# Two clearings on GpSimd ahead of its first load, and a shorter spin on TensorE

## The chip, the cores and the metric

The kernel runs on one core of one Trainium2 chip. A core has TensorE (PE, matrix products; PEld is its loading of stationary operands), VectorE (DVE), ScalarE (ACT), GpSimd (POOL) and SyncE (SP), and sixteen DMA engines that move data between the device's memory and the core. The metric is device microseconds from the first to the last instruction, as the median of repeated executions. Lower is better.

## The reference, cut to what matters

Eight batches of twelve heads with 448 rows of 64 elements go through an attention without softmax: the scores are scaled, negative ones are cut to zero, and the rest is squared. The heads, side by side, are the 3584 x 768 input of a two-layer network with an exact GELU.

```
scores = q @ k.T / sqrt(64)
attn   = maximum(scores, 0) ** 2 / 448
x      = (attn @ v) with the 12 heads side by side     # 3584 x 768
h      = x @ w_in                                      # 3584 x 2048
g      = 0.5 * h * (1 + erf(h / sqrt(2)))
out    = g @ w_out                                     # 3584 x 768
```

Inputs and output are float32; the kernel computes in bfloat16 with float32 sums.

## The kernel before, in words

Batches follow each other. For each, queries and keys are loaded and converted to bfloat16 (tiles `nq`, `nk`), transposed (`qT`, `kT`), multiplied to scores (line 623, tile `ps`), cut to zero (635 on ScalarE, 637 on VectorE) and squared (644), multiplied with V (683, `pav`), and copied as the network's input (`xT`). The first layer (line 730) ends in GELU on ScalarE (740), the second is at 1036 and 1131. Parts of both layers use Strassen's seven products in place of eight; their sums are formed on VectorE. Twelve heads are worked on in three groups of four.

The order of the work is fixed when the program is built. Operations are entered with durations and dependences in a planner (`Scheduler`), the first 270 placements are spelled out in the string `ORDER`, and the rest is placed by the planner; after the call of `manual_schedule` (line 1198) every engine runs its instructions in that order. No number of the planner is touched by the change. What is emitted before line 1198, the preamble that the change edits, is put in order by the framework.

Loads come in two kinds. Almost all are issued by GpSimd[...]. Batch 0 starts differently: the keys of its first head group (`k32`) are loaded as float32 by a DMA issued from ScalarE (line 1181), and half the queries of that group (`q32`) by one from SyncE (1182). ScalarE and VectorE then convert them (lines 387 and 389; in the profile the tiles stand as `k` and `q`). GpSimd's own loads start with the second group: K of group 1, half the queries of group 1, V of group 0, K of group 2, half the queries of group 2, V of groups 1 and 2, the other half of all queries, and then the first pieces of `w_in` (lines 1201 to 1208 enter them, lines 421, 336 and 439 issue them).

Ahead of that stands a preamble. A tile `zero` is cleared, a 128 x 128 identity `ident` is made for the transposes on TensorE (cleared on VectorE at line 1185, its diagonal set by GpSimd's select at 1186), ScalarE's GELU table is loaded with a dummy activation (1193), and TensorE multiplies `zero` by itself 45 times (1197, `SPIN`). These products have no reader; they keep TensorE active until the first data arrive. The transposes of keys are on line 517, those of queries on line 545. The pool `opool` has three buffers of 128 x 768 float32 under the tag `osb`, which hold output rows before they are stored.

Of the kernel before, what the change touches and what calls it, by code (L numbers as in the profile page):

```python
# [8 lines left out]
F32 = mybir.dt.float32  # L9
# [13 lines left out]
DM = H * D  # L23
# [41 lines left out]

COLD_END = 0.0
K_CUT = 4
SPIN = 45


ORDER = """
# [212 lines left out]
def kernel(  # L284
# [9 lines left out]
    nc = tc.nc  # L294
# [3 lines left out]
    def pool(name, bufs, space=None):  # L298
        if space is None:
            return ctx.enter_context(tc.tile_pool(name=name, bufs=bufs))  # L300
        return ctx.enter_context(tc.tile_pool(name=name, bufs=bufs, space=space))
# [11 lines left out]
    opool = pool("opool", 3)  # L313
# [58 lines left out]
    ident = const.tile([128, 128], BF16, tag="ident", name="ident")  # L372
# [10 lines left out]
    V, A = nc.vector, nc.scalar  # L383
# [785 lines left out]
    def slots(b, done):  # L1169
# [12 lines left out]
    nc.sync.dma_start(q32, q_view(0, 0, 1, 0, HC))  # L1182
    zero = const.tile([128, 128], BF16, tag="zero", name="zero")
    V.memset(zero, 0.0)
    V.memset(ident, 0.0)
    nc.gpsimd.affine_select(
        out=ident, in_=ident, compare_op=mybir.AluOpType.not_equal, fill=1.0,
        base=0, pattern=[[-1, 128]], channel_multiplier=1,
    )
    warm = const.tile([128, 1], F32, tag="warm", name="warm")  # L1190
    V.memset(warm, 0.0)

# [2 lines left out]
    spin = w_pp.tile([128, 2, NB], F32, tag="w", name="spin")  # L1195
    for _ in range(SPIN):
        nc.tensor.matmul(spin[:, 0, :128], zero, zero, start=True, stop=True)
# [187 lines left out]
```

## Time and profile before

| | before |
|---|---|
| time, median of 3 | 376.12 us (375.93 to 377.31) |
| span of the profiled execution | 374.2 us |
| TensorE busy | 363.0 us, 97% |
| VectorE busy | 284.3 us, 76% |
| ScalarE busy | 200.9 us, 54% |
| GpSimd busy | 46.0 us, 12% |
| HBM read, written | 45.61 MB, 11.01 MB |

The page gives the busy time of each engine, the span in 40 slices, the DMA queues, and the chain of waits: the work that ended last, followed backwards from the last instruction, at each step to what released it. In a timeline each line has the start in microseconds, the duration, the engine, the line of the code, the operation, what it writes and reads with its shape, and how often. In brackets at the end stands how long the engine was idle before, and what ended that. A table of windows gives, for each stretch of time, the busy time of the engines, then TensorE's granted clock, the busy share of the DMA engines, and the gigabytes per second that they moved.

### The profile page before, as it was taken

How to read it: one execution, taken by the hardware profiler on the slowest of the kernel's cores; microseconds unless marked ns; L12 is line 12 of the kernel's file. 1: busy time of each engine (PE TensorE's matmuls, PEld its weight loads, DVE VectorE, ACT ScalarE, POOL GpSimd, SP SyncE). 2: the span in 40 equal slices, each digit the busy share in tenths (PEclk: the TensorE clock that was granted, in tenths of full speed). 3: DMA queues.
4: the chain of work that ended last, by engine and by line, in shares of the span. 5: the costliest groups of instructions: out<-in, count | busy, mean ns of one | idle time of the engine just before them, and what ended most of it. 6: DMA issues, size and time to landing. Idle time of an engine off the chain costs nothing.

```text
span 374.2 us, 8324 instructions
## 1 busy us (share of the span) xinstructions
PE 363.0 (97%) x3485; PEld 215.4 (58%) x3485; DVE 284.3 (76%) x517; ACT 200.9 (54%) x301; POOL 46.0 (12%) x69
## 2 busy tenths in 40 slices
PE   8799999999999999999999999999999999999995
PEld 7566645455554455544555445544555886688663
DVE  3998981799848787985889768946888879785762
ACT  4998864746337865666546575657562333035100
POOL 8666400300002011002000020000000000000000
PEclk9999999999999999999999999999999999999999
DMA  9999999997579969989333799400020201210233
GB/s 175 195 201 204 202 190 114 171 205 143 94 171 162 146 75 190 238 113 159 64 101 79 140 154 181 120 3 0 2 86 12 75 2 31 90 49 2 85 86 84
DMA packets 69685, 42.96 MB, mean 115 GB/s; under 512 B 37776, under 2 KB 66192, under 8 KB 69648
## 3 DMA queue, kind: packets, MB, share of 16 engines
q0 software_dynamic: 30512, 22.47, 40.2%
q1 hardware_dynamic: 38768, 19.46, 25.5%
q8 instruction: 27, 0.44, 0.5%
q10 hardware_dynamic: 368, 0.51, 0.4%
q14 instruction: 10, 0.08, 0.1%
HBM read 45.61 MB, written 11.01 MB: 151 GB/s over the span
## 4 chain that ended last, share of the span: by engine, by line
PE 84%; DVE 6%; ACT 4%; issue 2%; DMA 2%; POOL 1%; DVEq 0%; ACTq 0%; POOLq 0%
PE pso L1036 32%; PE psh L730 29%; PE ps L623 8%; PE pb L870 7%; PE pav L683 4%; ACT a_sq L635 4%; PE pso L1131 3%; DVE a_sq L644 3%; DVE part L904 2%; DMA nk<-in_k_dram 2%; DVE a_sq L637 1%; DVE xT L387 0%; DVE kT L387 0%; PE tp L517 0%; ACT xT L389 0%
## 5 line engine op out<-in xcount | busy, mean ns | idle before, releaser
L635 ACT ACTIVATE a_sq<-ps 128x896 bf16<-128x896 f32 (+1 forms) x143 | 122.8, 914 | 57.5 <-PE ps L623 57.5
L730 PE MATMUL psh<-xT,win_sb 128*128 128x448 bf16 (+1 forms) x612 | 114.2, 342 | 0.1
L644 DVE TENSOR_TENSOR a_sq<-a_sq 128x896 bf16<-128x896 bf16 (+1 forms) x169 | 98.7, 615 | 11.2 <-ACT a_sq L635 10.1
L730 PEld LDWEIGHTS <-win_sb 128*128 128x128 bf16 x612 | 57.4, 98 | 53.7 <-issue 9.2
L740 ACT ACTIVATE h_sb<-psh 128x448 bf16<-128x448 f32 x96 | 52.5, 547 | 34.3 <-PE psh L730 34.0
L1036 PEld LDWEIGHTS <-s_sb 128*128 128x128 bf16 x424 | 40.6, 98 | 27.7 <-issue 2.5
L623 PE MATMUL ps<-qT,kT 64*64 64x448 bf16 (+1 forms) x756 | 48.5, 336 | 3.1 <-ACT a_sq L635 0.7
L637 DVE TENSOR_SCALAR a_sq<-ps 128x896 bf16<-128x896 f32 x26 | 28.2, 1088 | 28.5 <-PE ps L623 28.1
L1036 PEld LDWEIGHTS <-h_sb 128*128 128x128 bf16 x312 | 29.8, 98 | 20.9 <-issue 2.4
L1036 PE MATMUL pso<-wout_sb,h_sb 128*128 128x384 bf16 x208 | 38.1, 326 | 0.0
L1036 PE MATMUL pso<-t_sb,s_sb 128*128 128x384 bf16 x208 | 38.1, 326 | 0.0
L1036 PE MATMUL pso<-wout_sb,s_sb 128*128 128x384 bf16 (+2 forms) x216 | 38.1, 320 | 0.0
L683 PE MATMUL pav<-a_sq,v_sb 64*64 64x448 bf16 (+1 forms) x756 | 36.8, 330 | 0.8 <-ACT a_sq L635 0.4
L623 PEld LDWEIGHTS <-kT 64*64 64x64 bf16 x756 | 18.6, 105 | 26.9 <-issue 21.3
L1070 DVE TENSOR_TENSOR osb<-pso,p_sb 128x384 f32<-128x384 f32 x39 | 21.6, 555 | 9.5 <-PE pso L1036 7.3
L683 PEld LDWEIGHTS <-v_sb 64*64 64x64 bf16 x756 | 21.1, 107 | 13.1 <-issue 2.3
L387 DVE CAST xT<-pav 128x448 bf16<-128x448 f32 (+1 forms) x44 | 24.3, 582 | 5.5 <-PE pav L683 4.9
L904 DVE TENSOR_TENSOR part<-pb,part 128x448 f32<-128x448 f32 x40 | 23.1, 618 | 6.3 <-PE pb L870 6.2
L913 ACT ACTIVATE h_sb<-part 128x448 bf16<-128x448 f32 x24 | 13.3, 577 | 18.4 <-DVE part L904 18.3
L590 POOL COPY gate<-qT 128x4 bf16<-128x4 bf16 x5 | 1.3, 266 | 155.6 <-DMA qT<-pq 155.6
L870 PEld LDWEIGHTS <-win_sb 128*128 128x128 bf16 x192 | 18.4, 98 | 3.2 <-issue 2.1
L1036 PE MATMUL pso<-t_sb,h_sb 128*128 128x384 bf16 x104 | 19.0, 326 | 0.0
(60 smaller groups left out, 262.1 us busy)
## 6 DMA issues: line engine op xcount, KB each, us to landing
nk<-in_k_dram POOLq DMA_DIRECT2D x5, 672.0 KB, 6.7
nq<-in_q_dram POOLq DMA_DIRECT2D x5, 672.0 KB, 9.3
v_sb<-in_v_dram POOLq DMA_DIRECT2D x5, 672.0 KB, 13.4
out_dram<-osb SPq DMA_DIRECT2D x8, 336.0 KB, 3.1
wout_sb<-in_moe_w_out_dram POOLq DMA_DIRECT2D x2, 1152.0 KB, 11.7
v_sb<-in_v_dram POOLq DMA_DIRECT2D x9, 224.0 KB, 9.0
out_dram<-osb SPq DMA_DIRECT2D x7, 288.0 KB, 3.1
out_dram<-osb SPq DMA_DIRECT2D x8, 240.0 KB, 2.8
```

What stands on the lines that cost most here:

```text
L387: V.tensor_copy(dst, src)
L623: nc.tensor.matmul(ps[64 * j : 64 * j + 64, e, x * w : x * w + w], kT[r, g, i * 128 + 64 * j : i * 128 + 64 * j + 64], qT[r, 2 * g + j, co ...
L635: A.activation(ar, ps, AF.Relu, scale=c_att)
L637: V.tensor_scalar(ar, ps, c_att, 0.0, op0=mybir.AluOpType.mult, op1=mybir.AluOpType.max,)
L644: V.tensor_mul(box["a2"][:, :, :used], ar, ar)
L683: nc.tensor.matmul(pav[0][o2 : o2 + 64, e, :w], vt[b][r, 2 * g + e, bass.ts(i, D)], box["a2"][r, e, o : o + w], start=(i == 0), stop=(i == ...
L730: nc.tensor.matmul(ph[:, x * n : x * n + n], win_sb[:, kd, bass.ts(m + x, 128)], xT[b][:, kd, c], start=(kd == 0), stop=(kd == KD - 1),)
L740: A.activation(h_ring()[:, m : m + nm, o + c.start : o + c.stop], box[0][:, :S].rearrange("p (x n) -> p x n", x=nm), AF.Gelu,)
L870: nc.tensor.matmul(bank[name][:, y, z * HS : z * HS + HS], w[:, k, bass.ts(mm, 128)], right()[:, k], start=first and k == 0 and z == 0, st ...
L904: V.tensor_add(get(to), ps(name), get(other))
L1036: nc.tensor.matmul(box[bank][:, n0:n1], left()[:, kf], right[:, kf, n0:n1], start=bool(need) and kf == 0, stop=kf == K2 - 1, skip_group_ch ...
L1070: V.tensor_add(out()[:, n0:n1], box[bank][:, n0:n1], other()[:, n0:n1])
```

## The change

The identity is cleared on GpSimd instead of VectorE. After the identity is made, GpSimd also clears a 128 x 768 float32 tile that takes one of the three output buffers; nothing reads it. Since GpSimd works in order, its first load can only be issued after these instructions. The spin on TensorE has 37 products instead of 45. The aim is to leave the DMA engines at first to the two loads issued by ScalarE and SyncE, which the first transposes wait for, and to fit the spin to the arrival of their data.

```diff
-SPIN = 45
+SPIN = 37
...
     zero = const.tile([128, 128], BF16, tag="zero", name="zero")
     V.memset(zero, 0.0)
-    V.memset(ident, 0.0)
+    nc.gpsimd.memset(ident, 0.0)
     nc.gpsimd.affine_select(
         out=ident, in_=ident, compare_op=mybir.AluOpType.not_equal, fill=1.0,
         base=0, pattern=[[-1, 128]], channel_multiplier=1,
     )
+    first = opool.tile([128, DM], F32, tag="osb", name="osb")
+    nc.gpsimd.memset(first, 0.0)
```

## The prediction

> **What bounds the kernel now.** I read the page first: which engine is busy, and what ended the time before. Columns of the first two lines: busy time, share of the span, instructions; then busy tenths in 40 slices.
>
> ```profile
> PE 363.0 (97%) x3485; PEld 215.4 (58%) x3485; DVE 284.3 (76%) x517; ACT 200.9 (54%) x301; POOL 46.0 (12%) x69
> PE   8799999999999999999999999999999999999995
> ...
> PE 84%; DVE 6%; ACT 4%; issue 2%; DMA 2%; POOL 1%; DVEq 0%; ACTq 0%; POOLq 0%
> ```
>
> TensorE fills the span except at the two ends, so a change in the first 3 us can only move the beginning; what it moves there is carried by a nearly full TensorE to the end. So I went to the chain of waits for the first 30 us (start, length, what):
>
> ```profile
> 1.26 0.80 POOL nk L421
> ...
> 2.14 0.31 POOL ident L1186
> 2.45 0.67 POOL nq L336
> 3.12 0.69 POOL v_sb L439
> 3.81 5.92 DMA nk<-in_k_dram
> 9.73 0.04 issue
> 9.77 0.60 PE tp L517 x14
> 10.37 0.02 issue
> 10.40 0.62 DVE kT L387
> 11.02 2.98 DVE a_sq L644 x6
> ```
>
> The end hangs on the GpSimd loads: the fourth (K of the third head group, issued at 3.81) lands at 9.73, TensorE transposes it, VectorE copies it and then works without a gap. The other arm, the two float32 loads issued by ScalarE and SyncE, is off the chain. The timeline shows it:
>
> ```profile
> 0.99 4.98 PE L1197 MATMUL spin<-zero 128*128 128x128 bf16 x45 [0.99 <-DVE zero L1184]
> 1.24 0.81 POOL L421 DMA_DIRECT2D nk<-in_k_dram  x1 [0.79 <-POOLq L1369]
> ...
> 5.44 0.62 ACT L389 CAST nq<-q 112x512 bf16<-112x512 f32 x1 [2.70 <-DMA q<-in_q_dram]
> 5.64 0.56 DVE L387 CAST nk<-k 128x512 bf16<-128x512 f32 x1 [4.62 <-DMA k<-in_k_dram]
> ...
> 6.11 0.56 PE L545 MATMUL tp<-ident,nq 112*64 112x112 bf16 x8
> ...
> 9.77 0.58 PE L517 MATMUL tp<-ident,nk 128*64 128x128 bf16 x14 [0.53 <-DMA nk<-in_k_dram]
> ```
>
> Query data land at 5.44, the spin ends near 5.97, the first transposes start at 6.11; and at 9.77 TensorE has already waited 0.53 us for the fourth load. So two questions decide: does the GpSimd stream start later, and do the first two loads land sooner? Both are answered by the DMA traffic (last two columns: busy share, GB/s):
>
> ```profile
> 2.50:3.00 0.50, 0.50 (x8) 0.50 (x7) 0.00 (x0) 0.23 (x2) 0.50 (x1) 1.00 0.52 153
> 3.00:3.50 0.50, 0.50 (x7) 0.50 (x6) 0.00 (x0) 0.00 (x0) 0.50 (x2) 1.00 1.09 391
> 3.50:4.00 0.50, 0.50 (x8) 0.50 (x6) 0.00 (x0) 0.00 (x0) 0.50 (x2) 1.00 1.08 394
> 4.00:4.25 0.25, 0.25 (x5) 0.25 (x3) 0.00 (x0) 0.00 (x0) 0.25 (x1) 1.00 1.06 382
> 4.25:4.50 0.25, 0.25 (x6) 0.25 (x4) 0.00 (x0) 0.00 (x0) 0.25 (x2) 1.00 1.16 334
> 4.50:4.75 0.25, 0.25 (x5) 0.25 (x4) 0.00 (x0) 0.00 (x0) 0.25 (x2) 1.00 1.20 211
> ```
>
> 390 GB/s until 4.25 are the float32 loads, 200 GB/s afterwards are the converting GpSimd loads. The trace's packet records, split by queue, say it exactly: the first GpSimd packet starts at 4.32, and on engine after engine 6 ns after the last packet of the ScalarE load (4.316 then 4.322, 4.350 then 4.356, 4.428 then 4.434). Sixteen engines end those two loads between 4.31 and 4.86. From 4.32 to beyond 13.5 the GpSimd queue has no gap. When the engines are idle, a GpSimd load has its first packet 1.52 us after its issue begins (112.03 to 113.55, 139.57 to 141.11, 167.82 to 169.33, 214.91 to 216.43). The first load, issued at 1.24, took 3.08. So about 1.56 us of it was waiting behind the two other loads.
>
> [...] spin matmuls stand 107 ns apart, 8 query transposes take 0.56 us at 6.11 and 0.39 at 7.58, and the trace's clock record begins at 6.52.
>
> **The change part by part.**
>
> *Identity and clearing on GpSimd, ahead of its first load.* VectorE loses a 0.11 us clearing that nobody waits for at that time. GpSimd gains three pieces before its load.
> - Start: its first instruction of the kernel's body stood at 1.22; VectorE's at 0.82. I take 1.22, bound 0.82.
> - Clearing the identity: a one-element clearing takes 0.10; [...] Upper: the slope of the select, (0.311 - 0.098) / 127 = 1.68 ns, gives 0.31.
> - Building the identity: 0.31 plus 0.08 of set-up (2.06 to 2.14), 0.39, moved from after the load to before it.
> - Clearing 128x768 float32: [...] upper 0.10 + 768 x 1.68 ns = 1.39. I take 0.76.
>
> The first load so issues at 1.22 + 0.21 + 0.39 + 0.76 = 2.58; from 2.18 (start 0.82, low prices) to 3.31 (all high). Its first packet could come 1.52 later: 4.10, from 3.70 to 4.83. Today it comes at 4.32, because of the two other loads. So a hold until 2.80 costs the stream nothing, and mine ends 0.2 us before. Only the upper end is late, by 4.83 - 4.32 = 0.5.
>
> Queued behind it on GpSimd are all the other loads. The gap of 0.33 for the select between first and second (2.05 to 2.38) goes, so the fourth issues 0.81 + 0.74 + 0.71 = 2.26 after the first, at 4.84 against 3.81. Its first packet could be at 6.36; it starts at 7.45 today, behind its forerunners in the stream. The issue is hidden by the transfers.
>
> *What the hold can give.* If the early GpSimd load disturbs the two others, they land sooner without it. The packets leave little room: most engines were done with them by 4.5, the slowest at 4.86, so at best 0.4 of the landing. The gain reaches the end only where the fourth load also moves, since VectorE's order puts its copy (10.40) ahead of the squaring, and VectorE idled 0.37 before that copy. Bounds 0 and 0.4; I take 0.2.
>
> *Spin 45 to 37.* Eight times 0.107 is 0.86 us less: last one issued near 4.8, end near 5.1. Today TensorE then waits for the query cast anyway (ends 6.06), so nothing is gained unless the cast starts more than 0.3 earlier; the shorter spin makes room for that. It also opens an idle stretch of up to 1 us before 6.1 (a risk to the clock, below). The buffer cleared is one of three output buffers; its next writer comes after 80 us. Nothing.
>
> Sum: 376.12 + 0.0 (stream) - 0.2 (landing) = 375.9.
>
> **The rivals.**
> 1. *The hold is too long* (slower). For it: the large clearing is not in the trace, and GpSimd's first load gates the chain. At the upper prices the stream starts 0.5 late, and the wait at 9.77 grows by that: 376.6. Against: it needs 1.68 ns an element for a plain clearing.
> 2. *The clock is released later* (slower). For it: [...] TensorE's work between runs at half rate: K transposes +0.19 and +0.14, q +0.17, scores 24 x (187 - 93)/4 ns = +0.56, next K +0.36; 1.4 in all, less the 0.53 of waiting that it fills: +0.9, so 377.0. [...]
> 3. *The two loads were badly slowed* (faster). For it: between 2.0 and 2.75, [...] only 33 GB/s flow in the half microsecond from 2.0. If that is its doing, the loads (458 and 229 kB, 1.75 us at 392 GB/s, first packet at 1.79) could end before 4, and the stream would start as early as the hold lets it: 3.70 with the low price, 0.6 sooner, so 375.5. Against: the rate is full afterwards, and no GpSimd packet lies between theirs; and at 2.58 the hold itself gives back only 0.2.
>
> **How the numbers follow.** My forecast, hidden hold, gets 50%; too long 18%; late clock 12%; badly slowed loads 20%. All four lie within 0.5% (1.9 us) of 376.12. The outermost cases are 375.5 and 377.0. Single runs of the kernel before lie 1.4 apart (375.93 to 377.31); a median moves less, and I add 0.5 on either side: range 375.0 to 377.5. For a time outside 0.5%, which needs something that I don't see, faster 5%, slower 8%; same 87%.
>
> **What would show it.** In the profile after: GpSimd's clearing of 128x768 between 0.6 and 1.4 us, its first load issued between 2.2 and 3.3, about 2.6; the step from 390 to 200 GB/s again near 4.3, with no idle DMA between; the fourth load landing between 9.4 and 9.8; casts at 5.0 to 5.4; spin ending near 5.1. A dip in traffic near 4.5 shows rival 1; transposes of the first group as long as 0.56 us after 6.5 show rival 2; the 2.0 to 2.75 dip gone shows rival 3. I am wrong if the clearing takes over 2 us, if the select waits for something new, or if the start settles the order of later transfers in a way that the first 15 us don't show.

## The result, and the profile after

The changed kernel takes 377.77 us (median of 6, 377.45 to 378.75) against 376.12: 1.65 us more, ratio 1.0044 with an interval of 1.0026 to 1.0062. It is slower, and outside the forecast range of 375.0 to 377.5. The forecast was a small gain.

The page's 40 slices show the loss at the beginning, in TensorE's first slice (6, where it was 8) and in its granted clock there (8, where it was 9):

```profile
PE   6889999999999999999999999999999999999995
...
PEclk8799999999999999999999999999999999999999
```

The chain of waits of the changed kernel, to be laid beside the one of before:

```profile
0.88 0.75 POOL osb L1191
...
1.66 0.28 POOL ident L1186
1.94 0.77 POOL nk L421
...
4.13 6.76 DMA nk<-in_k_dram
...
10.94 0.97 PE tp L517 x14
...
11.94 0.62 DVE kT L387
12.56 1.90 DVE a_sq L644 x4
```

It is the same chain. The fourth load is issued 0.32 later (4.13 against 3.81) and lands 1.16 later (10.89 against 9.73). Its transposes take 0.97 instead of 0.60. Squaring begins at 12.56 against 11.02, 1.54 later; the last copy to `kT` before the first layer begins at 31.37 against 29.73, 1.64 later; the span is 1.6 longer. So nearly the whole difference is made before 12.6 us and carried to the end. TensorE's timeline before, then after:

```profile
7.58 0.39 PE L545 MATMUL tp<-ident,nq 112*64 112x112 bf16 x8
7.97 0.77 PE L623 MATMUL ps<-qT,kT 64*64 64x224 bf16 x24
```

```profile
5.72 0.39 PE L545 MATMUL tp<-ident,nq 112*64 112x112 bf16 x8 [1.05 <-ACT nq L389]
...
7.61 0.58 PE L545 MATMUL tp<-ident,nq 112*64 112x112 bf16 x8 [0.66 <-DMA nq<-in_q_dram]
8.13 1.33 PE L623 MATMUL ps<-qT,kT 64*64 64x224 bf16 x24
9.39 0.96 PE L517 MATMUL tp<-ident,nk 128*64 128x128 bf16 x14
10.94 0.96 PE L517 MATMUL tp<-ident,nk 128*64 128x128 bf16 x14 [0.59 <-DMA nk<-in_k_dram]
```

Two things are new. TensorE waits for loads at 7.61, where it didn't before. And between 7.46 and 14.29 it runs at half rate (the trace's clock record): the 24 score products take 1.33 instead of 0.77 (each four start 187 ns after the last four, instead of 96). The clock had been at full rate from 4.05 (spin products start 107 ns apart before it, 56 after). In the 3.41 us between 4.05 and 7.46 TensorE was busy for 1.59: it idled 1.05 us after the shorter spin, and 0.51 of the wait that ends at 7.61 lies there too.

The traffic shows where the loads went. Columns as before; the last is GB/s:

```profile
4.00:4.50 0.50, 0.50 (x11) 0.49 (x8) 0.00 (x0) 0.00 (x0) 0.50 (x2) 1.00 1.26 312
4.50:5.50 1.00, 0.17 (x4) 0.00 (x0) 0.29 (x1) 0.45 (x1) 1.00 (x2) 1.00 1.12 142
5.50:6.50 1.00, 0.61 (x16) 0.52 (x17) 0.69 (x2) 0.71 (x3) 1.00 (x3) 1.00 1.39 149
6.50:7.50 1.00, 0.36 (x6) 0.19 (x5) 0.40 (x2) 0.46 (x1) 1.00 (x2) 0.98 1.02 142
```

The GpSimd stream isn't late: its first packet is at 4.11, even 0.2 before the old 4.32. It is slow. From 4.5 to 10 us 147 GB/s flow instead of 196 (before, then after):

```profile
4.50:10.00 5.50, 4.51 (x90) 3.52 (x90) 3.29 (x6) 3.02 (x5) 5.09 (x8) 1.00 1.39 196
```

```profile
4.50:10.00 5.50, 3.53 (x70) 2.60 (x68) 2.86 (x5) 2.47 (x5) 5.42 (x8) 0.77 1.19 147
```

In the packet records most GpSimd packets of 896 bytes take 88 ns in both kernels, but in the changed one 51 GpSimd packets before 10 us take over 150 ns, up to 1422; before, it was 4. These are the "long packets" below.

### The profile page after: what moved, and what is told of

It is laid out like the page before. It is cut to its first block, busy times and chain, and to the rows that moved or that the text cites. A ratio compares the mean times of both kernels' runs of the same rounds, so it can differ in the third digit from the quotient of the medians.

```text
span 375.8 us, 8310 instructions
## 1 busy us (share of the span) xinstructions
PE 363.4 (97%) x3477; PEld 215.8 (57%) x3477; DVE 284.5 (76%) x516; ACT 201.1 (53%) x301; POOL 46.9 (12%) x71
## 4 chain that ended last, share of the span: by engine, by line
PE 84%; DVE 6%; ACT 4%; issue 2%; DMA 2%; POOL 1%; DVEq 0%; ACTq 0%; POOLq 0%
PE pso L1036 32%; PE psh L730 29%; PE ps L623 8%; PE pb L870 7%; PE pav L683 4%; ACT a_sq L635 4%; PE pso L1131 3%; DVE a_sq L644 3%; DMA nk<-in_k_dram 2%; DVE part L904 2%; DVE a_sq L637 1%; DVE xT L387 0%; PE tp L517 0%; DVE kT L387 0%; ACT xT L389 0%
## 5 line engine op out<-in xcount | busy, mean ns | idle before, releaser
L623 PE MATMUL ps<-qT,kT 64*64 64x448 bf16 (+1 forms) x756 | 49.6, 345 | 2.9 <-ACT qT L389 0.6
L623 PEld LDWEIGHTS <-kT 64*64 64x64 bf16 x756 | 19.4, 109 | 26.8 <-issue 21.2
L683 PEld LDWEIGHTS <-v_sb 64*64 64x64 bf16 x756 | 21.1, 107 | 12.6 <-issue 1.8
```

The lines of the kernel that those rows point to most:

```text
L623: nc.tensor.matmul(ps[64 * j : 64 * j + 64, e, x * w : x * w + w], kT[r, g, i * 128 + 64 * j : i * 128 + 64 * j + 64], qT[r, 2 * g + j, co ...
L683: nc.tensor.matmul(pav[0][o2 : o2 + 64, e, :w], vt[b][r, 2 * g + e, bass.ts(i, D)], box["a2"][r, e, o : o + w], start=(i == 0), stop=(i == ...
```

## The experiments

The theory after this comparison (stream, later called ramp): the later first load spoils the start of the GpSimd stream, and that costs most of the time. The rival (clock): the shorter spin does it, through the clock.

**One half of the change at a time.**

```diff
-SPIN = 45
+SPIN = 37
```

> Only the spin is shortened (37 products); the preamble on GpSimd is that of the kernel before. Theory stream (the later first load disturbs the GpSimd transfers, so that the fourth load lands at 10.9 instead of 9.7): nothing of it is in this kernel, so the fourth load lands at 9.6 to 9.8 and the time stays within 0.4 us of before. Theory clock (TensorE idles between the shorter spin and the first transposes, and its clock is halved until about 14 us): TensorE idles 1.0 to 1.3 us before 6.1, matmuls near 9 us take the half-rate times, and the time grows by 0.5 to 1.5 us.

Measured: ratio 1.0019 (1.0007 to 1.0031), 377.13 against 376.29. The stream was undisturbed (7 long packets), yet there is a loss, which the stream theory had not allowed. In the profile TensorE idles 1.15 before its first transposes at 6.27, and the clock record begins only at 10.42:

```profile
6.27 0.59 PE L545 MATMUL tp<-ident,nq 112*64 112x112 bf16 x8 [1.15 <-ACT nq L389]
...
8.48 1.33 PE L623 MATMUL ps<-qT,kT 64*64 64x224 bf16 x24
```

The 1.33 us are those of half rate again. Single executions spread from 375.69 to 378.65, more widely than those of before beside them (375.56 to 377.51): 7 of 20 stay at or below 376.4, of those of before 18 of 33.

The other half: the three edits on GpSimd with 45 spin products.

> Only the hold on GpSimd (identity cleared there, 128x768 cleared there); the spin has 45 products. Theory stream: GpSimd packets over 150 ns long between 4 and 10 us, fourth load landing at 10.5 to 11.1, time 1.0 to 1.6 us above before. Theory clock: no idle TensorE before 5.8, so the clock stays as before, the fourth load lands where it did, and the time is within 0.4 us of before or 0.2 below.

Measured: 1.0037 (1.0025 to 1.005), 377.64 against 376.29, with 35 long packets and the first issue at 1.90. The clock was at full rate from 5.99 on, so this loss of 1.35 needs no clock:

```profile
8.39 0.39 PE L545 MATMUL tp<-ident,nq 112*64 112x112 bf16 x8 [1.23 <-DMA nq<-in_q_dram]
8.71 0.77 PE L623 MATMUL ps<-qT,kT 64*64 64x224 bf16 x24
...
10.66 0.53 PE L517 MATMUL tp<-ident,nk 128*64 128x128 bf16 x12 [0.67 <-DMA nk<-in_k_dram]
```

The score products take 0.77, and the waits are for loads. Both theories hold a part: 1.35 for the hold, 0.84 for the spin, 1.65 for both. They don't add up; that a TensorE which is slower early waits less for the same landings would explain it, but no run shows it. The intervals of the hold alone and of the whole change overlap, so what the shorter spin adds on top of the hold isn't shown.

**What in the hold does it.** Without the clearing of the buffer, 45 spin products:

```diff
-    first = opool.tile([128, DM], F32, tag="osb", name="osb")
-    nc.gpsimd.memset(first, 0.0)
```

> The identity is cleared on GpSimd, the output buffer is not, and the spin has 45 products. The first load is then issued ahead of the select again, near 0.9 to 1.3 us. Theory stream: no disturbance, fourth load at 9.6 to 9.8, time within 0.4 us of before. If clearing on GpSimd as such (and not the moment of the first load) disturbs the stream: landing after 10.5 and over 1 us slower.

Measured: 1.0004 (0.9993 to 1.0015), first issue at 1.28, no long packet. Clearing the identity on GpSimd costs nothing. The framework put the load ahead of the select again, as expected, so this run doesn't test their order. With the buffer cleared twice:

```diff
     nc.gpsimd.memset(first, 0.0)
+    nc.gpsimd.memset(first, 1.0)
```

> As the hold alone, but the 128x768 tile is cleared twice, so that the first load is issued near 2.6 us [...]. Theory stream in the form 'descriptors that arrive while the ScalarE and SyncE loads run are the trouble': the disturbance gets smaller, fourth load at or before 10.3, under 0.8 us slower than before. In the form 'too few loads are described ahead when the stream starts': it gets larger, fourth load after 11, over 1.6 us slower.

Measured: 1.0043 (1.0026 to 1.006), 378.11 against 376.29, first issue at 2.58, 51 long packets, fourth load at 11.03. Of the two forms it is the second, nearly to the number: a still later issue, 2.58 with the first packet at 4.21, is no better, so the first form, which blames arriving during the float32 loads, gets no support. The clock has a part in this time: in the profile it ran at half rate from 8.02 to 14.85, with 45 products.

The trace of the kernel before holds the clue, at places I had used only for the first packet. There the DMA engines are idle when the first packet of a GpSimd load issued at 112.03 is due (an output store runs until 112.84; nothing runs ahead of the other three idle starts that the prediction names):

```profile
113.50:114.00 0.50, 0.50 (x7) 0.23 (x4) 0.28 (x1) 0.47 (x1) 0.50 (x2) 1.00 0.91 39
114.00:114.50 0.50, 0.50 (x4) 0.28 (x3) 0.50 (x1) 0.50 (x2) 0.50 (x1) 1.00 0.78 29
114.50:115.00 0.50, 0.50 (x7) 0.14 (x8) 0.50 (x2) 0.44 (x2) 0.11 (x1) 1.00 0.84 115
115.00:115.50 0.50, 0.50 (x9) 0.11 (x2) 0.50 (x2) 0.50 (x2) 0.00 (x0) 1.00 1.26 201
```

The first packet comes at 113.55, 1.52 after the issue, but for another microsecond only 29 to 39 GB/s flow, with packets of 300 to 950 ns. Full rate is reached about 3 us after the issue, at the other three places 3.0 to 3.5 us after it. The theory is now a ramp: a GpSimd stream needs 2.5 to 3 us from its first issue, and at the kernel's start the float32 loads hid all of it. The rivals tested next: the order of select and load, or the long clearing itself.

The select ahead of the load at nearly the old time, by clearing only 128 columns:

```diff
-    nc.gpsimd.memset(first, 0.0)
+    nc.gpsimd.memset(first[:, :128], 0.0)
```

> The hold with only 128 columns of the tile cleared, and 45 spin products: the select stands ahead of the first load as in the change, but the first load is issued near 1.3 us, as before the change. Theory ramp (a GpSimd load needs about 2.5 to 3 us from its issue until its packets flow at full rate; before the change the two float32 loads cover this, and every delay of the first issue uncovers it): packets stay at 88 ns, fourth load at 9.5 to 9.9, time within 0.4 us of before. Theory order (the select, or its set-up, ahead of the first load slows GpSimd's descriptors, whatever the time): long packets, fourth load after 10.4, over 0.9 us slower.

Measured: 0.9997 (0.9989 to 1.0005), first issue at 1.47 (0.17 later than I had expected), 5 long packets, fourth load at 9.57. The order doesn't matter. Now a late first load with no clearing on GpSimd; the kernel before plus:

```diff
     V.memset(warm, 0.0)
+    get_nat(0)
+    V.memset(nk[0][:, 2:4], 1.0)
```

> No clearing on GpSimd, 45 spin products: the first load waits for a VectorE write to its tile (about 0.9 us long) and is issued near 1.9 us, as in the change, without any extra work on GpSimd. Theory ramp: long packets from 4 to 9 us, fourth load at 10.4 to 11, 0.9 to 1.6 us slower, as with the hold alone. Theory clearing (a long GpSimd instruction ahead disturbs the descriptors or the tile's clearing does): no disturbance, within 0.4 us of before.

Measured: 1.0055 (1.0042 to 1.0068), 378.23 against 376.25, first issue at 2.27 (near 1.9 had been meant), 39 long packets, transposes of the fourth load at 11.29 after a wait of 1.92. A wait does the same as a clearing: it is the time of the first issue. Not all of the 1.98 us need be the stream's, since in this profile the clock was at half rate from 12.88 to 16.30. Then the ramp without cover and without a hold:

```diff
-    nc.scalar.dma_start(k32, kv_view(k, 0, 0, 1))
-    nc.sync.dma_start(q32, q_view(0, 0, 1, 0, HC))
+    V.memset(k32[:, :, :448], 0.5)
+    V.memset(q32, 0.5)
```

> Leaves out the two float32 loads of batch 0 (their tiles are filled with a constant on VectorE, so the first head group's scores of half the queries are not those of the inputs); GpSimd's first load is issued at 1.24 as before. Theory ramp: with nothing to hide behind, the first GpSimd packets come at 2.8, and for a microsecond or more only 30 to 100 GB/s flow, with packets of 200 to 1000 ns, though no hold is there. If the hold itself were the cause: packets of 88 ns and 200 GB/s from the first one on. The time itself says little, since the work on the first group can start sooner.

Measured: the first packet at 2.77, then the ramp in the open, with 68 long packets before 10 us (table of windows, GB/s last):

```profile
2.50:3.00 0.50, 0.50 (x6) 0.50 (x7) 0.50 (x1) 0.49 (x1) 0.50 (x2) 1.00 0.45 36
3.00:4.00 1.00, 1.00 (x12) 1.00 (x11) 0.06 (x1) 0.99 (x1) 0.92 (x3) 1.00 1.01 119
4.00:4.50 0.50, 0.50 (x8) 0.50 (x6) 0.00 (x0) 0.49 (x3) 0.50 (x1) 1.00 1.26 188
...
5.50:6.50 1.00, 1.00 (x12) 1.00 (x10) 0.00 (x0) 0.00 (x0) 1.00 (x2) 1.00 0.97 128
```

The stream gets near its rate 2.8 us after the issue, and then falls back: the slow stretch lasts until 9.5, which the 3.0 to 3.5 us of the idle starts don't explain. The changed kernel says the same in bytes. At 5.5 us, 3.6 us after its first issue, its GpSimd stream is 30 kB behind that of before; at 10 us it is 236 kB behind. With the hold alone it is 95 kB and 237 kB. So a start-up of 2.5 to 3 us accounts for the smaller part of the loss; the larger comes from a stream that stays slow after it.

The time, 377.72, says nothing here, since the fillings also delayed the spin to 2.47. A step between the harmless 1.47 and the harmful 1.90, by clearing 320 columns:

> The hold with 320 of the 768 columns cleared and 45 spin products: the first load is issued near 1.65 us, between the harmless 1.47 and the harmful 1.90. Theory ramp: some packets over 150 ns before 10 us (10 to 35, against at most 7 and at least 35), and 0.3 to 1.1 us slower than before. If there is no such scale and it is the length of the clearing that counts: as the 128 columns, within 0.3 us, or as the 768, over 1.2 us.

Measured: 1.0007 (0.9991 to 1.0022), first issue at 1.53 (0.12 earlier than I had meant), 3 long packets, where the theory had 10 to 35. The first packet came at 4.16, so in this profile 2.63 us after the issue are enough, where 2.33 (the hold alone) are not. The profile is of one of the faster executions, however: 4 of 12 took 377.43 to 378.18, of the kernel before beside them 3 of 31 took over 377.4. Whether the stream is already disturbed in some executions at this length stays open.

**More cover in place of less hold.** The hold with a third float32 load:

```diff
+    cover = opool.tile([128, DM], F32, tag="osb", name="osb")
+    nc.sync.dma_start(
+        cover, v[0].rearrange("h s d -> (h s d)")[: 128 * DM].rearrange("(p f) -> p f", p=128)
+    )
```

> The whole hold (first load issued near 1.9 us) with 45 spin products, and a third float32 load from SyncE, 393 kB into an output buffer that nobody reads, about 1 us more of traffic ahead of the GpSimd stream. Theory ramp: the stream starts near 5.1, over 3 us after its first issue, so its packets are all of 88 ns again (at most 10 over 150 ns before 10 us, and 195 GB/s or more from 5.5 to 10); the time is still about 0.8 to 1.4 us above before, now because of the late start. If the hold as such slows the stream: again 35 or more long packets, and over 2 us slower.

This run missed its purpose. With the load at this place the framework put GpSimd's first load ahead of select and clearing (1.27), so the hold came between the first and the second. Measured: 1.0035 (1.002 to 1.0049), 1 long packet, stream from 5.38. The repeat has the lines behind the clearing, and the first load is issued at 1.90:

> The whole hold ahead of the first GpSimd load (issued near 1.9 us), 45 spin products, and a third float32 load of 393 kB from SyncE into an output buffer that nobody reads, which keeps the DMA engines busy for 1 us more. Theory ramp: the stream starts near 5.3, 3.4 us after its first issue, and its packets are of 88 ns again: at most 10 over 150 ns before 10 us, 190 GB/s or more from 5.5 to 10, and a time within 0.4 us of the run with the same traffic and no hold. Theory hold-as-such: 35 or more long packets, and over 1 us slower than that run.

and its base is the kernel before with the extra load alone:

> The kernel before with the third float32 load and no hold: the first GpSimd load is issued at 1.24. Both theories: stream from about 5.3 at full rate, so about 1 us later than before the change, and a time of 0.8 to 1.4 us above before. If a stream that starts 1 us later costs less than 0.4 us, then the beginning of the stream isn't what sets the end, and the loss with the hold must have another way to the end.

Measured: hold and cover 1.0048 (1.0031 to 1.0066), 377.90; cover alone 1.0033 (1.002 to 1.0046), 377.55; both against 376.15. With cover the hold costs 0.35, which four and six executions don't tell from nothing, instead of 1.35; the whole is no faster, since the extra load costs 1.40. From 5.5 to 10 us the traffic is 190 GB/s, against 197 with cover alone and 162 with the hold alone. Long packets fall from 35 to 13, not to the 10 or fewer expected (0 with cover alone). The stream of the run with hold and cover, from 5.27 on:

```profile
5.50:6.50 1.00, 0.68 (x11) 0.42 (x10) 0.34 (x1) 0.88 (x2) 1.00 (x3) 1.00 1.16 186
6.50:7.50 1.00, 0.84 (x21) 0.73 (x18) 0.39 (x1) 0.41 (x2) 1.00 (x2) 1.00 1.53 181
```

So a later start takes most of the slowness away. It hides the start-up longer, and it also lets GpSimd issue more loads before the first packet moves (five by 5.27, against four by 4.23 with the hold alone); no run separates these two. The run with cover alone also prices a late stream: 1.1 us later (5.44 against 4.32) costs 1.40.

| kernel | first GpSimd issue | first packet | between | GpSimd packets over 150 ns before 10 us | ratio |
|---|---|---|---|---|---|
| before | 1.24 | 4.32 | 3.08 | 4 | 1 |
| no clearing | 1.28 | 4.42 | 3.14 | 0 | 1.0004 |
| 128 columns | 1.47 | 4.24 | 2.77 | 5 | 0.9997 |
| 320 columns | 1.53 | 4.16 | 2.63 | 3 | 1.0007 |
| changed kernel | 1.90 | 4.11 | 2.21 | 51 | 1.0044 |
| hold alone | 1.90 | 4.23 | 2.33 | 35 | 1.0037 |
| VectorE wait | 2.27 | 4.35 | 2.08 | 39 | 1.0055 |
| cleared twice | 2.58 | 4.21 | 1.63 | 51 | 1.0043 |
| no float32 loads | 1.24 | 2.77 | 1.53 | 68 | |
| hold and cover | 1.90 | 5.27 | 3.37 | 13 | 1.0048 |
| cover alone | 1.24 | 5.44 | 4.20 | 0 | 1.0033 |

**Is one landing the gate, or the stream?** Two loads exchanged in the kernel before (lines 1201 to 1205), K of group 2 ahead of V of group 0:

> The kernel before with one exchange in the order of GpSimd's loads: K of group 2 is issued third and V of group 0 fourth. If the landing of K of group 2 sets the end, as the chain of waits says, it lands about 1.1 us sooner, near 8.6, TensorE's wait at 9.77 goes, and 0.3 to 0.5 us are gained (VectorE idles 0.37 before the copy that follows). V of group 0 then lands near 9.7, 2 us before its first use. If something else ends equally late there, the time stays within 0.2 us.

Measured: 1.0003 (0.9996 to 1.001). The landing moved as expected, squaring began at 9.91 instead of 10.94, and then the gain went into the next wait for the same stream:

```profile
14.78 0.58 PE L545 MATMUL tp<-ident,nq 112*64 112x112 bf16 x16 [0.65 <-DMA nq<-in_q_dram]
...
20.41 0.58 PE L517 MATMUL tp<-ident,nk 128*64 128x128 bf16 x14 [0.69 <-DMA nk<-in_k_dram]
```

With the second half of the queries also ahead of V of group 2:

> The exchange of the run before, and the second half of all queries also issued ahead of V of group 2. The run before moved the fourth landing but gave its gain to a wait for the second half of the queries at 14.78 (0.65 us) and one for K of batch 1 at 20.41 (0.69 us). If single loads are the gates, this one removes the wait at 14.8 and gains 0.3 to 0.7 us. If the GpSimd stream as a whole is the bound of the first 20 us, the gain moves to the wait at 20.4, and the time stays within 0.3 us of before: then a stream that starts late costs its whole delay.

Measured: 0.9994 (0.9984 to 1.0003). The wait near 14.8 went, but the gain did not move to a wait at 20.4, as the second theory had it: no wait for a load is left on TensorE between 12 and 30 us. The chain of this profile has no GpSimd load in it any more. It begins with the float32 queries and goes on through VectorE and ScalarE:

```profile
0.74 4.82 DMA q<-in_q_dram
...
5.59 0.63 ACT nq L389
...
10.53 3.01 DVE a_sq L644 x6
```

Yet the time is that of before within its interval, which allows a gain of up to 0.6 us. So in the kernel before the GpSimd stream is hardly the only bound: the chain of the float32 queries and of VectorE's work on batch 0 would end nearly as late. Making the stream earlier shows no gain clear of noise, while making it later costs (1.40 with cover alone). I found no version that beats both kernels beyond its interval. The hold together with both exchanges, where the float32 loads are on the chain, was not tried.

**The spin once more**, with 29 products in the preamble of before:

> The preamble of the kernel before, with 29 spin products. Theory clock (the gap between the end of the spin and the first transposes makes a full-rate clock in the first 10 us a matter of luck): the gap grows to 2 us, fewer executions stay under 376.4 us than with 37 products (7 of 20 there), the median is 1.0 to 1.8 us above before. If the loss with 37 products had another cause than the gap: as there, 0.5 to 1.0 us above before.

Measured: 1.0022 (1.001 to 1.0034), 377.03 against 376.22, one execution of 13 at 376.4 or below. In the profile the clock reached full rate at 3.94, fell to half at 7.35 and came back at 10.76. The executions without loss got rarer, as the clock theory says (1 of 13 against 7 of 20, few to count on), but the median grew by 0.81, as with 37 products, below the 1.0 expected: on the size the rival's forecast came true.

Other profiles show that a gap after the spin is not enough to lose the clock. In the run that cleared 128 columns, with 45 products, the clock came as early as in the changed kernel (3.98), the spin was through at 5.08, and TensorE idled longer before its first transposes:

```profile
6.21 0.39 PE L545 MATMUL tp<-ident,nq 112*64 112x112 bf16 x8 [1.13 <-ACT nq L389]
```

The clock stayed full, and no time was lost. There TensorE was busy for 2.02 of the 3.41 us from 3.98 on, in the changed kernel for 1.59 of those from 4.05 on, where 0.51 of a wait for a late load fell into the same stretch. With the buffer cleared twice and 45 products a wait of 1.02 for a load did, and the clock fell as well. So late loads may have a part in the fall of the clock in the changed kernel, and it can't be laid to the shorter spin alone. Nor is there one limit of busy time: with both exchanges 1.88 of the 3.41 us kept the clock, while in the run with the shorter spin alone it fell again, at 20.66, after 2.23.

## Why the prediction was wrong, step by step

**What bounds the start.** Right: the landing of the GpSimd loads. Too narrow: I took the fourth landing for the gate. With it earlier, later loads of the stream took its place (waits at 14.78 and 20.41), and with those earlier too, the float32 queries and VectorE's work did.

**The price of the hold.** I put the first issue at 2.58, with bounds of 2.18 and 3.31; it came at 1.90, below both. The prices of the two clearings in its sum, 0.21 and 0.76, were my estimates, which nothing in the trace of before shows; the changed kernel's trace has 0.20 and 0.74. But the first instruction started at 0.74, not 1.22, and neighbours overlap: start to start are 0.14 for the identity's clearing, 0.78 for the buffer's, 0.24 for the select.

**The step that failed: "So a hold until 2.80 costs the stream nothing."** In the sum this was the term "0.0 (stream)"; the hold alone measured +1.35. The step equated readiness with the first packet, 1.52 after the issue. The first packet did come in time, at 4.11, but the stream behind it stayed slow until about 10 us. In the profiles 2.63 us between first issue and first packet were enough and 2.33 were not, so the free hold ended between 1.53 and 1.90, and even the shorter hold of the real kernel overran it. I had named the idle starts at 112 and 139 us and read from them one number instead of the rate behind it. After the issue at 112.03 the first packet came after 1.52 us, and 201 GB/s only about 3 us after it.

**The landing of the float32 loads.** It happened: queries at 5.05 instead of 5.44, and from 4.99 to 5.13 in four profiles with a first GpSimd load at 1.90 or later and no extra traffic, against 5.34 to 5.69 in seven of the eight comparable ones with an early one. The eighth had 5.05 with an early load, so the early load doesn't always cost them. (Of the sixteen engines seven were done with the two loads by 4.5, not most of them as the prediction says; all but one were by 4.69.) The gain of 0.2 at the end did not follow: nothing on the chain waits for these two loads, and the fourth load, which I had made its condition, came later.

**The spin.** "Nothing is gained" was right, "nothing is lost" wrong. Rival 2 had the late clock and nearly the size (+0.9): with the shorter spin alone TensorE idled 1.15 before its first transposes, the record begins at 10.42 instead of 6.52, and +0.84 was measured. Its sum counts TensorE's work until then at half rate, and for the 24 score products the price came out as there (1.33 - 0.77 = 0.56). That the idle stretch delays the clock was my estimate; no run shows it as the cause, and with 128 columns 1.13 of it left the clock at full rate. In the changed kernel the clock was not late but lost again at 7.46, in a stretch that held a wait for a late load too. I gave this rival 12% as an alternative to a hold that is too long (18%), and ended the range short of both together; the 1.35 of the hold alone, on top of 376.12, already reaches its end (377.47 of 377.5).

**The rivals.** Rival 1 (hold too long) had the right direction and gate and the wrong form. Its sign, a dip near 4.5, came (142 GB/s from 4.5 to 5.5), but the stream was not late, and it stayed slow long after. Rival 3 was right that the two loads speed up (121 GB/s from 2.0 to 2.5 us, where it was 33) and wrong that it counts; that the early GpSimd load held the rate down there was my estimate.

What stays open: why a stream that starts too soon after its first issue stays slow until about 10 us, when the idle ones recover within 3.5 us of the issue. One rival is untested. The slow stretch ends about where GpSimd's first unbroken series of issues does (at 9.93 in the changed kernel, at 9.64 without the float32 loads), so GpSimd's issuing of further loads (0.72 to 0.82 us each for the first five of the changed kernel) may disturb a stream that follows it closely; against it, the kernel before issues until 9.59 without harm. Open too are why 13 long packets are left with hold and cover, and what decides when the clock reaches full rate and when it loses it.

## What to carry to other kernels

When a stream of GpSimd loads starts behind other traffic, ask how much time lies between its first issue and its first packet, and don't shorten it untested. From a start on idle engines in the same trace read when the full rate is reached, not when the first packet comes, and after a change compare the rate over the next 5 us. An early issue that seems to do nothing but wait may be worth its place: the hold alone, 1.90 instead of 1.24, cost 1.35. A spin's end is no spare time, even if TensorE then waits for data: eight products fewer cost 0.84 us here. Whether a gap after it loses the clock differed from profile to profile, so compare medians of many executions.

## What the runs showed of the hardware that was not expected

- A GpSimd load on idle DMA engines (kernel before, issue at 112.03): first packet after 1.52 us, 29 to 39 GB/s for the next microsecond, 200 GB/s after about 3 us.
- In the four profiles with float32 loads and 1.63 to 2.33 us between first issue and first packet, 35 to 51 GpSimd packets before 10 us took over 150 ns (up to 1.42 us in the changed kernel; 4 before), and from 4.5 to 10 us 144 to 155 GB/s flowed instead of 196.
- TensorE's clock record in the changed kernel, at full rate from 4.05, went to half at 7.46, after 3.41 us in which TensorE was busy for 1.59 and never idle for more than 1.05 us on end, and stayed so for 6.8 us.
- An idle stretch of 1.13 us in the same place (128 columns cleared, TensorE busy for 2.02 of 3.41 us) left the clock at full rate.
